# Releasing the first weight matrix earlier, moving one pair's keys and queries between the two weight loads, and summing keys on VectorE

## The chip, the cores and the metric

The kernel runs on one core of one Trainium2 chip. The metric is the device time of one execution in microseconds (us); lower is better. A profiled execution gives the span from the first to the last instruction, and the traces of the engines: TensorE (PE, with its weight loads as PEld), VectorE (DVE), ScalarE (ACT), GpSimd (POOL) and SyncE (SP), and of the DMA queues.

## The reference

Block-sparse causal attention is followed by a two-layer MLP with a GELU. Four batches (b), 8 heads, 768 positions, head size 64; the MLP takes 3072 rows of 512, with 2048 hidden columns.

```
k_rep = mean of k over blocks of 64 keys                  # 12 block means per head
gate  = q . k_rep, future blocks -1e9
sel   = the 3 best blocks of each query, and its own block
attn  = softmax(where(sel & causal, q.k / 8, -1e9)) . v
x     = attn, heads side by side                          # 3072 x 512
out   = gelu_tanh(x @ w_in) @ w_out                       # 512 -> 2048 -> 512
```

## The kernel before

Two heads make a *pair*; there are 16 pairs, numbered p = 0 to 15, four to a batch. For each pair the kernel loads keys, queries and values (k, q, v; 384 KB each), forms key sums of the 12 blocks, computes gate scores on TensorE, finds the third best with VectorE's MAX8 (`sel_e`), turns the result into an additive mask (`mask`, `mc`), multiplies keys with queries in six units per pair (`st_e`), takes exponentials on ScalarE (`ex_e`), zeroes the part above the diagonal on GpSimd (`af_e`), and multiplies with the values on TensorE (`pv_e`). Sums and quotients give `xn`, which is transposed to `xT`. When four pairs are through, the batch's MLP runs: `s1` (x times w_in, GELU into `G`) and `s2` (G times w_out). Batch 0 uses `pre` with transposes by TensorE and `heads2`; its second MLP half is `s2_plain`, 96 plain matmuls. Later batches use transposes by VectorE (`tr`) and `heads`.

Keys of batch 0 are transposed by TensorE into a PSUM bank (`turn`, lines 545 and 548). For the pairs named in `KSUM` (0 and 1 before) the transposing matmul against `identk` has 130 columns rather than 128, and the two more give the block sums; `ksb_h` then only has to multiply them with a mask. For the other pairs of batch 0, `ksb_h` has VectorE add up the transposed keys in the bank (TENSOR_REDUCE, line 583) before the mask.

Loads. SP issues nearly all loads, in one queue and in order. Batch 0's k, q and v come first; then come four `fill`s (8 small copies into `kT`), then `hold`, a copy of a few bytes out of the end of w_in into `after_in` (line 1567), which makes SP wait until w_in has landed; then the loads of pair 4 (k and q in four DMAs each, 96 KB each, line 400) and on. The two weight matrices are issued by POOL (`load_w`, line 460), two DMAs each. Ahead of w_in's stands a small copy by POOL that reads the v of pair 3, and so holds w_in back until that v has landed. w_out's two DMAs have no such copy before; they stand later in POOL's order.

Order. Every step is an `add`ed operation with a number. `ORDER` is a list of all numbers and is emitted as it stands, so it fixes each engine's own sequence. It was found ahead of time by a search over a plan with costs; `BUFFER` gives the PSUM and SBUF buffers in the order of use, and `ENGINE` moves single copies to ACT or POOL. `warm` operations (line 1524) are matmuls of zeros that nothing reads; a few of them stand wherever the plan had left TensorE unoccupied. An engine runs its own instructions strictly in order, so a wait of one holds up all behind it.

Of the kernel before, what the change touches and what calls it, by code (L numbers as in the profile page):

```python
# [189 lines left out]
    "POOL": [  # L190
        586, 587, 646, 647, 707, 972, 973, 1035, 1036, 1097, 1098,
        1159, 1160, 1425, 1489, 1551, 1612]}


class Op:
# [1431 lines left out]
```

## Time and profile before

| what | value |
|---|---|
| median of 3 runs | 257.9 us (257.89 to 257.94) |
| span of the profiled execution | 256.0 us |
| around the span (median less span) | 1.9 us |
| PE busy | 246.5 us, 96% of the span |
| DVE busy | 191.4 us, 75% |
| ACT busy | 176.4 us, 69% |
| POOL busy | 84.3 us, 33% |
| w_in issued, landed | 26.97, 41.55 us |
| first matmul with w_in, with w_out | 38.45, 50.31 us |

Times in the profile count from the first instruction. The page gives busy times of whole engines; the windows cut the span into stages; the timeline lists instructions with their start, duration, engine and line, and in square brackets the idle time before one and what ended it. The span is one execution and the median is of three others, so sums are made against the span, and what lies around it is added at the end.

### The profile page before, as it was taken

What the parts mean: (1) busy time and instruction counts of PE and PEld (TensorE: products, weight loads), DVE (VectorE), ACT (ScalarE), POOL (GpSimd) and SP (SyncE); (2) the same over time, 40 slices, a digit from 0 to 9 for tenths busy, and PEclk for the clock granted to TensorE, in tenths of its full rate; (3) what the DMA queues carried; (4) which work ended last, traced back from release to release, by engine and by line L of the source; (5) the groups of instructions that cost most, each with busy time, mean ns of one, the idle gap of its engine ahead of it and who ended that gap; (6) DMA issues with size and microseconds to landing.
All of it is one profiled execution on the core that took longest, in us unless ns stands there. A gap on an engine that the chain in (4) does not pass through costs nothing.

```text
span 256.0 us, 6451 instructions
## 1 busy us (share of the span) xinstructions
PE 246.5 (96%) x2485; PEld 171.2 (67%) x2485; DVE 191.4 (75%) x539; ACT 176.4 (69%) x225; POOL 84.3 (33%) x163
## 2 busy tenths in 40 slices
PE   7889999999998999999899999999999999999994
PEld 5667686555554566555578888555777786766883
DVE  2769751041989889989999999699889665579954
ACT  2399997634898998667969884566889957557300
POOL 8465970000239366223053853100056620000000
PEclk9999999999999999999999999999999999999999
DMA  8997599999989995999899699532112520040024
GB/s 164 218 208 166 94 212 191 213 161 157 184 142 165 153 143 99 172 179 199 127 174 110 144 188 166 118 94 69 26 34 72 64 74 1 3 165 0 3 82 164
DMA packets 130927, 32.62 MB, mean 127 GB/s; under 512 B 124528, under 2 KB 126928, under 8 KB 130896
## 3 DMA queue, kind: packets, MB, share of 16 engines
q1 hardware_dynamic: 126160, 27.62, 65.4%
q0 software_dynamic: 3136, 4.19, 9.7%
q10 hardware_dynamic: 1600, 0.39, 0.8%
q8 instruction: 19, 0.31, 0.5%
q14 instruction: 12, 0.10, 0.1%
HBM read 27.26 MB, written 6.29 MB: 131 GB/s over the span
## 4 chain that ended last, share of the span: by engine, by line
PE 51%; DVE 16%; SPq 11%; DMA 10%; POOL 4%; issue 3%; ACT 3%; ACTq 1%; DVEq 0%; POOLq 0%
PE bank L1372 17%; PE wide L1122 10%; SPq L400 9%; PE wide L1046 6%; PE wide L1211 5%; DMA w_in<-in_moe_w_in_dram 5%; PE bank L1085 5%; PE bank L1322 3%; DVE qT L367 3%; DMA sd<-in_k_dram 3%; DVE sel L719 2%; DVE s L564 2%; DVE XS L1309 2%; DMA G<-in_q_dram 2%; ACT ats L882 1%
## 5 line engine op out<-in xcount | busy, mean ns | idle before, releaser
L1122 PE MATMUL wide<-xT,w_in 128*128 128x384 f16 x416 | 72.6, 326 | 0.0
L1059 ACT ACTIVATE ats<-wide 128x896 f16<-128x896 f32 x72 | 63.4, 915 | 8.9 <-PE wide L1046 6.2
L1134 ACT ACTIVATE G<-wide 128x768 f16<-128x768 f32 x52 | 42.1, 810 | 27.3 <-PE wide L1122 27.0
L1122 PEld LDWEIGHTS <-w_in 128*128 128x128 f16 x416 | 40.0, 98 | 26.8 <-issue 1.3
L1073 POOL TENSOR_SCALAR_AFFINE_SELECT ats<-ats 128x256 f16<-128x256 f16 x72 | 33.3, 475 | 60.3 <-ACT ats L1059 60.2
L1046 PE MATMUL wide<-qT,kT 76*128 76x512 f16 (+3 forms) x192 | 39.1, 305 | 0.1
L564 DVE STREAM_TRANSPOSE s<-sd 128x768 f32<-128x768 f32 x24 | 23.1, 968 | 18.7 <-DMA sd<-in_k_dram 17.2
L1372 PE MATMUL bank<-w_out,G 128*128 128x256 f16 x216 | 31.4, 272 | 0.0
L1372 PEld LDWEIGHTS <-G 128*128 128x128 f16 x288 | 26.9, 98 | 6.0 <-issue 0.3
L1322 PE MATMUL bank<-w_out,G 128*128 128x512 f16 x96 | 28.1, 379 | 0.0
L365 POOL CAST kT<-s 64x768 f16<-64x768 f32 x17 | 15.2, 891 | 37.5 <-DVE s L564 37.0
L1421 DVE TENSOR_TENSOR osb<-bank,osb 128x512 f32<-128x512 f32 (+1 forms) x38 | 22.1, 592 | 5.1 <-PE bank L1372 4.5
L1085 PEld LDWEIGHTS <-ats 128*128 128x128 f16 x504 | 22.2, 98 | 3.9 <-POOL ats L1073 0.4
L1085 PE MATMUL bank<-v,ats 128*128 128x65 f16 x504 | 24.4, 194 | 0.2 <-POOL ats L1073 0.2
L1046 PEld LDWEIGHTS <-kT 76*128 76x128 f16 x192 | 17.3, 98 | 10.5 <-issue 0.8
L1372 PEld LDWEIGHTS <-XS 128*128 128x128 f16 x216 | 20.0, 98 | 5.5 <-DVE XS L1309 1.5
L1372 PE MATMUL bank<-TS,XS 128*128 128x256 f16 x144 | 22.0, 272 | 0.8 <-DVE XS L1309 0.7
L882 ACT ACTIVATE ats<-wide 128x1024 f16<-128x1024 f32 (+3 forms) x24 | 20.8, 924 | 1.3 <-PE wide L863 0.8
L365 POOL CAST v<-vsd 128x768 f16<-128x768 f32 x13 | 11.4, 875 | 13.8 <-DMA vsd<-in_v_dram 8.8
L969 DVE TENSOR_TENSOR xn<-bank,zr 128x384 f16<-128x384 f32 x24 | 13.4, 558 | 0.8
L719 DVE MAX8 sel<-sel 128x8 f32<-128x12 f32 x160 | 13.2, 158 | 0.6
L1322 PEld LDWEIGHTS <-G 128*128 128x128 f16 x96 | 8.9, 98 | 6.1 <-issue 0.3
(120 smaller groups left out, 358.6 us busy)
## 6 DMA issues: line engine op xcount, KB each, us to landing
out_dram<-osb SPq DMA_DIRECT2D x23, 256.0 KB
vsd<-in_v_dram SPq DMA_DIRECT2D x26, 192.0 KB
sd<-in_k_dram SPq DMA_DIRECT2D x48, 96.0 KB
sd<-in_q_dram SPq DMA_DIRECT2D x48, 96.0 KB
w_in<-in_moe_w_in_dram POOLq DMA_DIRECT2D x2, 1024.0 KB, 11.5
w_out<-in_moe_w_out_dram POOLq DMA_DIRECT2D x2, 1024.0 KB, 14.5
G<-in_k_dram SPq DMA_DIRECT2D x4, 192.0 KB
G<-in_q_dram SPq DMA_DIRECT2D x4, 192.0 KB
```

The source lines that it names most:

```text
L365: nc.gpsimd.tensor_copy(out=out, in_=in_)
L400: nc.sync.dma_start(out=T[key, p][64 * hh + 32 * a:64 * hh + 32 * a + 32], in_=SRC[key][b, 2 * hp + hh].rearrange("(t i) (a j) -> a i t j" ...
L564: nc.vector.transpose(out=T[key + "T32", p], in_=T[key, p].rearrange("p t j -> p (t j)"))
L882: nc.scalar.activation(out=T["at", u][:, :, 0:n], in_=plan.buf[("st",) + u].rearrange("p (h w) -> p h w", h=2)[:, :, 0:n], func=AF.Exp, bi ...
L1046: nc.tensor.matmul(st[:, x:e], kT16[i][h][0:76, s0:s0 + 128], qT16[i][h][0:76, s0 + (x - cb):s0 + (e - cb)], start=True, stop=True)
L1059: nc.scalar.activation(out=T["at", u][:, 0:n], in_=plan.buf[("st",) + u][:, 0:n], func=AF.Exp, bias=0.0, scale=SCALE)
L1073: nc.gpsimd.affine_select(out=dg, in_=dg, compare_op=ALU.is_ge, fill=0.0, base=0, pattern=[[0, 2], [1, 128]], channel_multiplier=-1)
L1085: nc.tensor.matmul(pvv[:, qc, 0:65], at[:, cb + (qc - jc) * 128: cb + (qc - jc + 1) * 128], v16[i][:, jc, h, :], start=(gi == 0 and jc == ...
L1122: nc.tensor.matmul(hps[:, 512 * e:512 * e + HALF], w_in16[:, ci, (2 * j + e) * 128: (2 * j + e + 1) * 128], T["xT", b][:, ci, HALF * h:HAL ...
L1134: nc.scalar.activation(out=G[:, :, h, j, :], in_=plan.buf["hps", b, j, h].rearrange("p (e w) -> p e w", e=2)[:, :, 0:HALF], func=AF.Gelu_a ...
L1322: nc.tensor.matmul(plan.buf["ops", b, ti], G[:, f % 2, 2 * ti // NC, f // 2, ti % (NC // 2) * 128:ti % (NC // 2) * 128 + 128], w_out16[:, ...
L1372: nc.tensor.matmul(dst[:, HD * h:HD * h + HD], FACT[m][0][:, j, t * 128:(t + 1) * 128], FACT[m][1][:, j, :], start=(clear and j == 0), sto ...
```

## The change

There are four edits.

1. `KSUM` becomes empty: keys of pairs 0 and 1 are transposed with 128 columns, and VectorE adds up their blocks, as for pairs 2 and 3.
2. w_in's copy on POOL reads the v of pair 2 rather than that of pair 3.
3. The loads go w_in, k and q of pair 4, w_out, v of pair 4, and on, rather than w_in, w_out, k, q, v of pair 4. `load_w` now puts a copy ahead of w_out too: it reads the q of pair 4, so that POOL issues w_out when that q has landed.
4. `ORDER`, `BUFFER` and `ENGINE` are searched anew.

```
-    KSUM = (0, 1)
+    KSUM = ()
...
-            if name == "in":
-                nc.gpsimd.tensor_copy(out=x, in_=T[after][96:97, 0, 1, 0:16])
+            src = T[after]
+            nc.gpsimd.tensor_copy(
+                out=x, in_=src[96:97, 0, 1, 0:16] if len(src.shape) == 4 else
+                src[96:97, 0, 0:16])
             for part in parts:
                 nc.gpsimd.dma_start(out=dst[part], in_=view[part])
...
-    for x in ('in', 'out', ('k', HP + 0), ('q', HP + 0), ('v', HP + 0), ('k', HP + 1), ('q', HP + 1), ('v', HP + 1)):
+    for x in ('in', ('k', HP), ('q', HP), 'out', ('v', HP), ('k', HP + 1), ('q', HP + 1), ('v', HP + 1)):
...
-            load_w(x, dst, src, parts, [ld[prev]] if x == "in" else
-                   [after_w["in", 0]], prio, prev)
+            load_w(x, dst, src, parts, [ld["v", 2], *chain] if x == "in"
+                   else [ld[prev], after_w["in", 0]], prio, ("v", 2) if x == "in" else prev)
```

What the new lists do, as read from the two orders side by side:

- SP's first DMA is half of pair 1's q (192 KB), ahead of pair 0's k. Of batch 0's loads, q and v of pair 3 come last, behind the v of pair 2.
- POOL: w_in's copy stands behind the cast of pair 1's v and ahead of the diagonal steps of pair 1 (before: behind the cast of pair 2's v). The cast of pair 3's v stands between diagonal steps of pair 2, with one of pair 2 and all four of pair 3 behind it. w_out's copy stands behind the last diagonal step of batch 0; after it come a cast of pair 4's k and steps of pairs 4 and 5.
- ACT: of the copies between the first and the last exponential of batch 0 there are 5 rather than 8; the others went to VectorE or ahead of the first exponential. One copy of `xT` behind the last exponential went to VectorE.
- TensorE: 72 `warm` matmuls rather than 39; 58 stand ahead of the first matmul of `s1` (before: 26), 13 from there to the MLP of batch 1, and 1 behind the last real matmul. The first `s1` group is one that needs w_in's second half (before: its first). 47 groups of `s1` (two matmuls each), the gate and the mask of pair 4, two `pv_e` steps of pair 3 and 4 warm matmuls stand ahead of the first `s2_plain` matmul.

More of the change, by code (lines that the diff above doesn't have):

```diff
@@ L21 @@
 ORDER = [
[134 rows of a table removed]
-BUFFER = [
[24 rows of a table removed]
[131 rows of a table added]
+BUFFER = [
[25 rows of a table added]
 ENGINE = {
     "ACT": [
[5 rows of a table removed]
[5 rows of a table added]
     "POOL": [
-        586, 587, 646, 647, 707, 972, 973, 1035, 1036, 1097, 1098,
-        1159, 1160, 1425, 1489, 1551, 1612]}
+        338, 587, 646, 647, 707, 708, 972, 973, 1035, 1036, 1097, 1098,
+        1159, 1160, 1425, 1426, 1488, 1489, 1551, 1612]}
 class Op:
```

324 rows, old and new, of tables (BUFFER, ENGINE, ORDER) are left out of this document.

## The prediction

> **What bounds the kernel now.** I read the page first, then the windows by stage, then the timeline at each stage's border.
>
> ```profile
> span 256.0 us, 6451 instructions
> PE 246.5 (96%) x2485; PEld 171.2 (67%) x2485; DVE 191.4 (75%) x539; ACT 176.4 (69%) x225; POOL 84.3 (33%) x163
> ...
> GB/s 164 218 208 166 94 212 191 213 161 157 184 142 165 153 143 99 172 179 199 127 174 110 144 188 166 118 94 69 26 34 72 64 74 1 3 165 0 3 82 164
> ```
>
> ```profile
> 12.50:38.45 25.95, 24.93 (x441) 18.59 (x441) 19.12 (x75) 23.97 (x34) 18.30 (x33) 1.00 0.95 170
> 38.45:69.60 31.15, 31.15 (x198) 17.79 (x196) 10.27 (x27) 18.95 (x26) 1.65 (x2) 1.00 1.22 182
> 69.60:101.66 32.06, 30.83 (x357) 18.36 (x354) 29.25 (x83) 29.10 (x37) 17.89 (x34) 1.00 0.93 140
> 101.66:135.00 33.34, 32.41 (x262) 20.90 (x259) 31.35 (x97) 24.26 (x33) 10.25 (x15) 1.00 1.18 169
> 160.00:252.70 92.70, 92.42 (x847) 67.71 (x844) 71.08 (x173) 57.54 (x69) 15.16 (x28) 1.00 0.25 63
> ```
>
> Each row has a stage, its length, and the busy time of PE, PEld, DVE, ACT and POOL. From 38.45 us on TensorE hardly rests: it is idle for 0, 1.23 and 0.93 us in the next three stages. So work on other engines counts only where it makes TensorE wait, and the change can win in two ways: `s1` starts earlier than 38.45, or one of those idle times goes. Until 38.45 the bound is another: ScalarE works 23.97 of 25.95 us, and what ends the stage is its last exponential.
>
> ```profile
> 12.50 1.03 ACT L882 ACTIVATE ats<-wide 128x1024 f16<-128x1024 f32 x1
> 34.82 3.26 ACT L882 ACTIVATE ats<-wide 128x1024 f16<-128x1024 f32 x4 [0.43 <-POOL ats L908]
> 38.45 1.79 PE L1122 MATMUL wide<-xT,w_in 128*128 128x384 f16 x10
> ```
>
> The exponentials of batch 0 run from 12.50 to 34.82 + 3.26 = 38.08 us, and `s1` follows at 38.45.
>
> The third thing to see is when the weights move.
>
> ```profile
> 23.50:28.50 5.00, 4.77 (x93) 3.61 (x92) 3.54 (x16) 4.98 (x8) 4.00 (x8) 1.00 0.13 30
> 28.50:40.50 12.00, 11.91 (x209) 9.02 (x210) 7.59 (x23) 10.62 (x15) 7.54 (x13) 1.00 1.10 191
> 52.50:69.00 16.50, 16.50 (x104) 9.07 (x103) 8.91 (x25) 9.00 (x12) 1.65 (x2) 1.00 1.17 172
> ...
> 25.94 0.83 POOL L365 CAST v<-TS 128x768 f16<-128x768 f32 x1
> 26.83 0.19 POOL L458 COPY after_in<-vsd 1x16 f32<-1x16 f32 x1
> 26.97 1.66 POOL L460 DMA_DIRECT2D w_in<-in_moe_w_in_dram  x2
> 34.74 1.78 POOL L460 DMA_DIRECT2D w_out<-in_moe_w_out_dram  x2
> ...
> 27.89 13.66 DMA w_in<-in_moe_w_in_dram
> 41.60 0.58 SPq L1567
> 43.41 2.70 SPq L400
> 46.15 3.21 SPq L400
> 49.40 2.79 SPq L400
> 53.12 0.54 SPq L400
> 53.70 0.52 SPq L400
> ...
> DMA to landing us min/median/max: 9.4/11.5/13.7
> ```
>
> The first three rows end in the DMA share and GB/s: for 5 us, until w_in moves, the queues carry 30 GB/s, then 191. w_in's two DMAs land 9.4 and 13.7 us after their issue, the second at 27.89 + 13.66 = 41.55. SP waits for that in `hold` and issues pair 4's keys only then, while w_out fills the queues: three of these DMAs of 96 KB hold SP for 2.70, 3.21 and 2.79 us, where one takes 0.54 once w_out is through. VectorE meanwhile has nothing to do:
>
> ```profile
> 54.40 0.98 DVE L564 STREAM_TRANSPOSE s<-sd 128x768 f32<-128x768 f32 x1 [14.96 <-DMA sd<-in_k_dram]
> 57.34 0.98 DVE L564 STREAM_TRANSPOSE s<-sd 128x768 f32<-128x768 f32 x1 [0.18 <-DMA sd<-in_q_dram]
> 69.64 0.90 ACT L1059 ACTIVATE ats<-wide 128x896 f16<-128x896 f32 x1
> 81.74 0.45 PE L756 MATMUL bank<-ident,madd 128*128 128x128 f16 x5 [1.20 <-DVE madd L724]
> ```
>
> It stands idle for 15 us before pair 4's keys come; at 69.60 to 101.66 it is busy 29.25 of 32.06 us, and TensorE's one long wait there (1.20 us at 80.5) is for pair 6's selection on VectorE.
>
> **Key sums on VectorE.**
>
> ```profile
> L583 DVE TENSOR_REDUCE ks<-bank 128x6 f32<-128x384 f32 x4 | 2.2, 550 | 0.8 <-ACT XS L363 0.8
> L545 PE MATMUL bank<-identk,G 128*128 128x130 f32 x24 | 3.5, 283 | 0.0
> L548 PE MATMUL bank<-identk,TS 128*128 128x128 f32 x12 | 1.7, 282 | 0.0
> 56.27 0.71 PE L1524 MATMUL bank<-XS 128*128 128x256 f16 x5
> 56.81 0.38 PE L1322 MATMUL bank<-w_out,G 128*128 128x512 f16 x1
> ```
>
> VectorE gets four more reductions of 0.55 us, 2.2 us in all. TensorE gets 12 transposes (1.7 us) for 24 matmul records (3.5), so it saves 1.8, and gets 33 warm matmuls at (56.81 - 56.27)/5 = 0.108, 3.6 us. Both lie nearly all ahead of `s1`, where TensorE is not the bound. On the path lie two of the reductions (1.1 us), and SP's first DMA, which puts pair 0's keys back by about 192 KB at 164 GB/s, 1.2 us. Against that, the first exponential of before stood behind copies on ScalarE that waited for VectorE's masked sums (2.1 and 1.6 us in the row quoted next). Bounds for the first exponential: 0.5 us earlier to 1.5 later; I take 0, since ScalarE's queue has slack there before and TensorE does the next transposes under the wait.
>
> **Batch 0's exponentials.** Three of ScalarE's eight copies between the first and the last exponential are gone:
>
> ```profile
> L363 ACT CAST XS<-bank 128x384 f16<-128x384 f32 x7 | 3.3, 490 | 4.3 <-DVE ksbx L595 2.1 <-DVE ksb L595 1.6 <-DVE ks L583 0.6
> ```
>
> 3 x 0.49 = 1.5 us at most; consecutive ones overlap a little, so I take 1.4. VectorE, which has 25.95 - 19.12 = 6.8 us to spare in the stage, hides them. With that cover gone (its chain to pair 3's mask is as long as ScalarE's) the gain is 0, and with pair 1's diagonals waiting behind w_in's copy on POOL it could be 1 us lost. Term: -1.4, between -1.9 and +1.0.
>
> **w_in.** All loads of batch 0 are through by 23.5. Pair 3's q and v (768 KB) now come behind pair 2's v, and at the page's 218 GB/s that is 3.6 us, so pair 2's v is moved at about 19.9; seen by POOL between then and 23.2 (the same 3.6 us ahead of the old copy at 26.83, rounded). I take 21.3, because the old copy stood behind a cast and not at the landing. Issue at 21.4 instead of 26.97 puts w_in's end at 41.55 - 5.5 = 36.0; sharing the queues with the last of pair 3's v and the fills costs perhaps 0.8, so 36.8. `s1` wants it at 38.45 - 1.4 = 37.05, now with its second half first. So the earlier w_in brings nothing by itself, but without it the 1.4 us would be lost: at the late bound (23.2) it lands at 38.7 and nothing is won. POOL's steps behind the waiting copy (pair 1's diagonals) wait until 23 us; the products that need them are due at about 23.5.
>
> By a rule of the Trainium skill ("SBUF — State Buffer", section "SBUF: two separate sides") a DMA issued from GpSimd has its descriptors written by GpSimd's cores, which are locked out while VectorE runs an operation that takes both ports; that speaks against issuing w_in in a stretch where VectorE works. The rows give 1.66 us for w_in's issue and 1.78 for w_out's, a difference of 0.12, and do not show such a lock. It is priced as a rival below.
>
> **Pair 4's keys and queries, then w_out.** `hold` ends at 36.8 + 0.6 = 37.4. Eight DMAs of 96 KB without w_out beside them take 0.55 to 0.85 each, 5.6 in all, to 43.0; the old queries landed at 57.2, 3 us behind their last issue with values behind them in the queue; at 172 GB/s the 768 KB take 4.6 us. So q lands at 44.5 to 46; I take 45.3. w_out is issued at 45.5; by w_in's 9.4 and 13.7 us its halves land at 54.9 and, from the second issue 0.9 later, 60.1. TensorE reaches the first `s2_plain` after 47 groups of `s1`; these cost 2 x 0.1624 each:
>
> ```profile
> 40.24 10.24 PE L1122 MATMUL wide<-xT,w_in 128*128 128x384 f16 x62
> 50.31 0.38 PE L1322 MATMUL bank<-w_out,G 128*128 128x512 f16 x1
> 66.69 2.10 PE L1322 MATMUL bank<-w_out,G 128*128 128x512 f16 x9
> 68.64 0.55 PE L1046 MATMUL wide<-qT,kT 76*128 76x512 f16 x3
> ```
>
> (50.31 - 40.24)/62 = 0.1624, so 15.3 us; gate, mask, two transposes, two products and four warm ones between them I estimate at 2.0 (the warm ones are 0.43 of it). 37.05 + 17.3 = 54.35, and w_out's first half is 0.6 us late. Term +0.6, from 0 to +6. The ninth `s2_plain`, the first to need the second half, comes 13 groups (4.2) and eight of (68.64 - 66.69)/9 = 0.217 later, 60.9: in time. In before, w_out was needed at 50.31 and TensorE did not wait.
>
> **The middle.** VectorE transposes and sums pair 4 at 42 to 47 us rather than 54 to 59, and the exponentials of batch 1 start at about 65 instead of 69.64 (60.9, four more groups of `s1`, and some 2.5 for the last GELU and the change of table), so the wait of 1.20 us for pair 6's selection should shrink; I take -1.0, from -1.2 to +1.0, as the search gives no promise of a new wait. Batch 1's sums: of 0.93 idle I take -0.3, from -0.9 to +0.8. After 160 us nothing is to be had: 0.28 us of idle time.
>
> **Sum.** 256.0 - 1.4 + 0.6 - 1.0 - 0.3 = 253.9; the median stands 1.9 above the span, so **255.8 us**, 0.8% below 257.9. About 0.2% (0.5 us) is what a measurement can tell from no change.
>
> **Rivals.**
> *w_out too late (slower).* Place: TensorE at its first `s2_plain`. POOL's copy waits for the queries, and each us that they land after 45 is one us of TensorE. It turns the gain at 47.4, where the wait is 2.7. If three of the eight DMAs take 3 us again (rows at 43.41 to 49.40), they land at 52, w_out's half at 61.5, the wait is 7: 256.0 - 1.4 + 7 - 1.3 + 1.9 = 262; halfway it is 259. For it: 0.6 us are missing already and all orders are fixed. Against: those rows are slow because w_out moved beside them. 0.20.
> *Pair 3's values starved (slower).* If w_in's packets start while over 200 KB of that v are left, these move at 96 KB in 3 us beside it and land after 29; POOL stands at the cast with the diagonals of pairs 2 and 3 behind it, and `s1` starts 3 to 5 us late: 259.5. For it: the same rows; against: the 3.6 us of q and v fit in POOL's way to the first packet. 0.08.
> *ScalarE isn't the bound ahead of `s1`.* The chain to pair 3's mask on VectorE, 2.2 us longer, keeps `s1` at 38.4; then -1.4 and +0.6 go: 256.0 - 1.3 + 1.9 = 256.6, or with the middle unchanged 257.9, so 257.5. 0.15.
> *Descriptors late.* If VectorE's work holds up both issues of w_in by 0.8 us each, `s1` waits 1.4 and w_out follows: 257.2 to 257.6. 0.07. By the Trainium skill's rule above this is what would happen; the trace so far bears it out only by 0.12 us.
> *All waits go.* 256.0 - 1.9 - 1.2 - 0.9 + 1.9 = 253.9. 0.08.
>
> **Numbers.** The forecast has 0.42 with a range of its own of 254.6 to 257.2. Faster: 0.42 + 0.08 + 0.04 from the two middle rivals, 0.54. Same: 0.14, nearly all theirs. Slower: 0.28 and 0.04 of theirs, 0.32. The range 253.8 to 259.6 leaves out the upper half of late w_out and some of the starved values at one end, a few hundredths at the other.
>
> **What would show it.** First exponential at 12 to 14 us, last one's end near 36.7; w_in issued at 21 to 22 and landed before 37.1; `s1` near 37; pair 4's keys at 0.55 to 0.85 us an issue; w_out issued near 45.5; TensorE idle at about 54 for less than 1 us; batch 1's first exponential near 65; `s1` of batch 1 near 100. The prediction is wrong if ScalarE idles over 2.5 us ahead of its last exponential, if TensorE waits over 2.7 us ahead of `s2_plain`, or if new idle time after 101 eats the rest.

## The result, and the profile after

The changed kernel takes 259.1 us (median of 13 runs) where the kernel before takes 257.8 in the same session: ratio 1.0058, 95% interval 1.0036 to 1.008. It is 0.6% slower; the prediction had it 0.8% faster. In a second session the ratio was 1.0058 again (1.0039 to 1.0077). The runs of the changed kernel spread over 258.1 to 260.9 us, those of before over 257.5 to 258.6.

The profiled execution of the changed kernel takes 259.66 us, 0.6 us above the median, and its span is 1.9 us longer than that of before. Its page and its windows, in the stages that the prediction used (length, then busy time of PE, PEld, DVE, ACT and POOL):

```profile
span 257.9 us, 6488 instructions
PE 249.0 (97%) x2506; PEld 172.8 (67%) x2506; DVE 193.0 (75%) x537; ACT 180.6 (70%) x228; POOL 85.8 (33%) x167
```

```profile
12.50:38.45 25.95, 25.15 (x429) 18.44 (x427) 21.26 (x87) 21.73 (x29) 14.94 (x25) 1.00 1.03 182
38.45:69.60 31.15, 31.15 (x238) 18.67 (x237) 13.76 (x35) 20.63 (x28) 4.55 (x8) 1.00 1.14 161
69.60:101.66 32.06, 32.03 (x361) 19.30 (x359) 25.39 (x77) 29.38 (x36) 17.21 (x33) 1.00 0.93 137
101.66:135.00 33.34, 33.05 (x264) 21.21 (x263) 31.71 (x93) 26.79 (x36) 11.86 (x18) 1.00 0.90 159
135.00:160.00 25.00, 24.10 (x307) 19.63 (x306) 22.03 (x43) 19.33 (x23) 11.97 (x24) 1.00 0.79 156
```

In the first row ScalarE works 21.73 us, 2.2 less than before, and VectorE 21.26, 2.1 more: the copies and sums moved as meant (the row is a fixed stretch of time; from the first exponential to the end of the last, ScalarE works 22.65 us instead of 23.61). In the third TensorE no longer rests (1.23 us before), in the fourth it rests 0.29 us (0.93 before); in the fifth 0.90 us of idle time are new in this execution. So the middle did what it should. The loss is ahead of all that. The timeline of ScalarE and TensorE of the changed kernel:

```profile
13.77 1.02 ACT L882 ACTIVATE ats<-wide 128x1024 f16<-128x1024 f32 x1 [0.30 <-PE wide L863]
39.32 1.30 ACT L882 ACTIVATE ats<-wide 128x256 f16<-128x256 f32 x2 [0.44 <-PE wide L863]
40.26 0.49 PE L1122 MATMUL wide<-xT,w_in 128*128 128x384 f16 x2
101.25 0.49 PE L1122 MATMUL wide<-xT,w_in 128*128 128x384 f16 x2
```

The first exponential comes at 13.77 (12.50 before), the last ends at 40.62 (38.08), `s1` starts at 40.26 (38.45; 37.05 was forecast). `s1` of batch 1 starts at 101.25, 0.41 us ahead of before: from one to the other the change gains 2.2 us. Now the start. TensorE's timeline of before, and then of the changed kernel; L545 and L548 are the transposes, L1524 the warm matmuls, L687 the first gate:

```profile
2.11 2.30 PE L1524 MATMUL bank<-XS 128*128 128x256 f16 x10
4.25 0.91 PE L545 MATMUL bank<-identk,G 128*128 128x130 f32 x6
4.99 0.49 PE L548 MATMUL bank<-identk,G 128*128 128x128 f32 x3
6.95 0.32 PE L687 MATMUL bank<-s,ksb 128*32 128x64 f32 x8
```

```profile
5.49 0.87 PE L548 MATMUL bank<-identk,G 128*128 128x128 f32 x3 [1.25 <-DMA G<-in_q_dram]
6.15 1.92 PE L1524 MATMUL bank<-XS 128*128 128x256 f16 x8
7.86 0.85 PE L548 MATMUL bank<-identk,G 128*128 128x128 f32 x3
8.50 1.06 PE L1524 MATMUL bank<-XS 128*128 128x256 f16 x4
9.35 0.95 PE L548 MATMUL bank<-identk,G 128*128 128x128 f32 x6
10.35 0.32 PE L687 MATMUL bank<-s,ksb 128*32 128x64 f32 x8
```

Read the rate from start to start. In before, three transposes take from 4.99 to 5.32, 0.11 us each. In the changed kernel TensorE waits 1.25 us for pair 0's queries, and behind that three transposes take from 7.86 to 8.50, 0.21 us each, and eight warm matmuls from 6.15 to 7.86, 0.21 each: half rate, until about 9.6 us. Before reached full rate at 4.3. Twelve warm matmuls at half rate stand between the transposes that the first gate needs; the gate is 3.4 us later than before's. The half rate was not in the prediction at all.

### The profile page after: what moved, and what is told of

Read it like the earlier page. It is cut to its first block, busy times and chain, and to the rows that moved or that the text cites. A ratio compares the mean times of both kernels' runs of the same rounds, so it can differ in the third digit from the quotient of the medians.

```text
span 257.9 us, 6488 instructions
## 1 busy us (share of the span) xinstructions
PE 249.0 (97%) x2506; PEld 172.8 (67%) x2506; DVE 193.0 (75%) x537; ACT 180.6 (70%) x228; POOL 85.8 (33%) x167
## 4 chain that ended last, share of the span: by engine, by line
PE 80%; DVE 13%; ACT 2%; DMA 2%; issue 1%; POOL 0%; ACTq 0%; DVEq 0%
PE wide L1122 24%; PE bank L1372 18%; PE wide L1046 9%; PE bank L1322 8%; PE bank L1085 5%; PE wide L1211 5%; DVE XS L1309 2%; PE wide L863 2%; DVE sel L719 2%; PE bank L687 2%; PE bank L1524 2%; PE bank L931 2%; DMA G<-in_q_dram 2%; DVE sel L710 1%; PE bank L548 1%; PE bank L988 1%
## 5 line engine op out<-in xcount | busy, mean ns | idle before, releaser
L1122 PE MATMUL wide<-xT,w_in 128*128 128x384 f16 x416 | 73.7, 326 | 0.0
L1134 ACT ACTIVATE G<-wide 128x768 f16<-128x768 f32 x52 | 42.0, 809 | 25.6 <-PE wide L1122 25.5
L1073 POOL TENSOR_SCALAR_AFFINE_SELECT ats<-ats 128x256 f16<-128x256 f16 x72 | 32.0, 457 | 54.0 <-ACT ats L1059 50.0
L1372 PE MATMUL bank<-w_out,G 128*128 128x256 f16 x216 | 32.2, 272 | 0.9 <-DVE osb L1421 0.9
L1372 PEld LDWEIGHTS <-G 128*128 128x128 f16 x288 | 27.0, 97 | 7.6 <-issue 1.2
L1322 PE MATMUL bank<-w_out,G 128*128 128x512 f16 x96 | 28.1, 379 | 0.0
L363 POOL CAST kT<-s 64x768 f16<-64x768 f32 x20 | 17.3, 865 | 20.1 <-DVE s L564 19.7
L1372 PE MATMUL bank<-TS,XS 128*128 128x256 f16 x144 | 22.6, 272 | 0.1
L1524 PE MATMUL bank<-XS 128*128 128x256 f16 x72 | 17.1, 326 | 1.1 <-DVE ks L302 1.1
L703 DVE STREAM_TRANSPOSE sel<-bank 128x160 f32<-128x160 f32 (+2 forms) x17 | 5.5, 330 | 14.7 <-PE bank L687 14.5
## 6 DMA issues: line engine op xcount, KB each, us to landing
out_dram<-osb SPq DMA_DIRECT2D x23, 256.0 KB
```

The costliest lines, as they stand in the source:

```text
L363: nc.gpsimd.tensor_copy(out=out, in_=in_)
L1073: nc.gpsimd.affine_select(out=dg, in_=dg, compare_op=ALU.is_ge, fill=0.0, base=0, pattern=[[0, 2], [1, 128]], channel_multiplier=-1)
L1122: nc.tensor.matmul(hps[:, 512 * e:512 * e + HALF], w_in16[:, ci, (2 * j + e) * 128: (2 * j + e + 1) * 128], T["xT", b][:, ci, HALF * h:HAL ...
L1134: nc.scalar.activation(out=G[:, :, h, j, :], in_=plan.buf["hps", b, j, h].rearrange("p (e w) -> p e w", e=2)[:, :, 0:HALF], func=AF.Gelu_a ...
L1322: nc.tensor.matmul(plan.buf["ops", b, ti], G[:, f % 2, 2 * ti // NC, f // 2, ti % (NC // 2) * 128:ti % (NC // 2) * 128 + 128], w_out16[:, ...
L1372: nc.tensor.matmul(dst[:, HD * h:HD * h + HD], FACT[m][0][:, j, t * 128:(t + 1) * 128], FACT[m][1][:, j, :], start=(clear and j == 0), sto ...
```

## The experiments

Each ran beside the kernel before on one chip; the ratio is to that, with its interval. "First selection" is the end of pair 0's first `madd` on VectorE (9.65 in before, 12.28 in the changed kernel). Starts and ends (of `s1`, say) are read from one profiled execution; times are medians over several.

**The start: late keys, warm matmuls or the rate?** `k0_first`, a move in SP's order:

```
 ORDER of the changed kernel
-    0, 22, 1890, 1891, 9, ... 1, 1902, 12, 1903, 71,
+    0, 1890, 1891, 9, ... 1, 1902, 12, 22, 1903, 71,
```

> The changed kernel with pair 0's keys first in SP's queue and the first half of pair 1's queries behind them, nothing else moved. Theory A (the start is late because the first keys are): pair 0's keys are turned about 1 us earlier, the first exponential comes at about 12.8 instead of 13.77 us, s1 at about 39.2 instead of 40.26, and the time is 258.0, 1.0 below the changed kernel's. Theory B (VectorE's key sums are the start's and the stage's limit): the keys come earlier but the sums of pairs 0 to 3 remain, s1 gains 0.4 at most, time 258.7. Theory C (warm matmuls stand ahead of TensorE's steps): nothing moves, 259.1.

258.3 us, 1.003 (1.0009 to 1.005). TensorE waited only 0.34 us ahead of its first transpose, ran at full rate from 4.8 us, the first selection ended at 9.42 and `s1` started at 38.39, earlier than theory A expected. But both the keys and the rate had changed, and the time fell by less than `s1` did. TensorE's timeline of it shows the next wait:

```profile
4.57 0.58 PE L548 MATMUL bank<-identk,G 128*128 128x128 f32 x3 [0.34 <-DMA G<-in_q_dram]
56.90 0.38 PE L1322 MATMUL bank<-w_out,G 128*128 128x512 f16 x1 [1.19 <-DMA w_out<-in_moe_w_out_dram]
```

`few_warm` takes warm matmuls out:

```
 ORDER of the changed kernel
-    44 warm numbers, 1904 to 1947 (from the first transpose to s1)
```

> The changed kernel without 44 of the 58 warm matmuls ahead of s1; the 14 ahead of its first transpose stay. Theory C (warm matmuls hold up TensorE's steps): they cost 44 times 0.11 to 0.2 us, so some of ScalarE's 4.5 us of idle time behind the units' matmuls goes; s1 about 1.5 earlier, 257.6. Theories A and B: they only fill time in which TensorE waits; s1 within 0.3 of 40.26, 259.1. Third case: without them the granted clock falls below 1.00 in the first 12 us or later, and s1 comes 1 us or more later, 260.

259.38 us, 1.0079 (1.0064 to 1.0093). With nothing to fill its waits TensorE stayed at half rate until 12 to 13.5 us. Yet `s1` came at 39.31, 0.95 us earlier, as no half-rate warm matmul stood ahead of the needed ones; the first `s2_plain` then waited 1.20 us for w_out. So theory C has a part in it, and the third case's lower rate too, and neither alone is the cause.

`bridge` keeps the late keys and all warm matmuls, and only moves ten of them:

```
 ORDER of the changed kernel
-    12, 1903, 71, 1904, 15, 23, 1905, ...
+    12, 1903, 1904, 1905, ... 1913, 71, 15, 23, ...
```

> The changed kernel with ten of its warm matmuls moved from behind the first transposes to ahead of them, so that TensorE works through the 1.25 us in which it waited for pair 0's queries; SP's order is the changed kernel's. Theory A1 (TensorE ran at half rate until 9.6 us because it had stood idle from 4.03 to 5.49; 128-column transposes 0.213 us from start to start there, 0.109 behind it): full rate comes by 6 us, the first gate at about 8.6 instead of 10.35, the first exponential near 12.0, s1 near 38.8; time 258.2. Theory A2 (only the late keys count, the rate does not): the first gate stays within 0.5 us of 10.35, s1 near 40, time 259.

258.5 us, 1.0032 (1.0011 to 1.0052). TensorE's timeline of it, the exponentials', and `s1`:

```profile
2.11 3.30 PE L1524 MATMUL bank<-XS 128*128 128x256 f16 x19
5.59 0.96 PE L548 MATMUL bank<-identk,G 128*128 128x128 f32 x6 [0.18 <-DMA G<-in_q_dram]
8.54 0.32 PE L687 MATMUL bank<-s,ksb 128*32 128x64 f32 x8
11.97 1.02 ACT L882 ACTIVATE ats<-wide 128x1024 f16<-128x1024 f32 x1 [0.29 <-PE wide L863]
37.90 0.49 PE L1122 MATMUL wide<-xT,w_in 128*128 128x384 f16 x2
56.74 0.38 PE L1322 MATMUL bank<-w_out,G 128*128 128x512 f16 x1 [1.52 <-DMA w_out<-in_moe_w_out_dram]
```

The data come no earlier (5.59), but full rate was there at 4.3, the first gate at 8.54, the first exponential 1.8 us and `s1` 2.36 us earlier, as A1 said. SP's order costs through the wait that it opens and what stands behind that wait: `k0_first`, with data 1 us earlier, has `s1` 0.5 us later than `bridge`. Two things changed at once, though: the wait is closed, and ten warm matmuls no longer stand between the needed transposes. The time falls by 0.3% only; in this profile w_out is now late by 1.52 us.

`after_again` is the changed kernel once more, for a second profile.

> The changed kernel, unaltered, beside the two below on one chip. If TensorE's rate at the start is what makes its runs spread (258.1 to 260.9): in this profile half rate ends between 9 and 10 us again where TensorE waited over 1 us for pair 0's queries, with s1 at 40 to 40.5 and a time of 259 to 260; in an execution whose half rate ends by 7 us, s1 is at 38 to 39 and the time 258.1 to 258.5. If the rate isn't it: s1 near 40.3 whichever it is.

259.29 us, 1.0058. Half rate to 9.2 us behind a wait of 1.32 us, first selection at 12.18, `s1` at 40.82: the first profile was no exception. No profile of an execution near 258.1 was had, so whether the spread of the times comes from the moment of full rate is not shown.

`before_gap` puts the fault into the kernel before:

```
 ORDER of before
-    1898, 1899, 1900, 1901, 1902, 1903, 1904, 62,
+    1898, 62,
```

> The kernel before without the last six of the 15 warm matmuls ahead of its first transpose, so that TensorE stands idle for the 1.28 us from 2.96 to 4.25, as it did for 1.25 us in the changed kernel; nothing else differs, and no data come later. Theory A1 (the idle time itself keeps TensorE at half rate): 128-column transposes stay at 0.213 us until 7 to 9.5 us (4.3 in before), the first gate is 1.0 to 1.5 us later than 6.95, and whatever of it the wait for VectorE at 8.5 to 9.7 does not swallow reaches s1: first selection (madd) up to 1.2 us later than 9.65, time 257.9 to 259.0. Theory A2 (the rate is not a matter of that idle time): half rate ends at 4 to 5.7 us as in the other runs of before's start, first gate within 0.3 us of 6.95, 257.7.

258.06 us, 1.0013 (1.0004 to 1.0022). TensorE's timeline of it (with a shorter list, its lines stand seven higher: L538 and L541 are the transposes, L680 the gate):

```profile
4.47 1.64 PE L538 MATMUL bank<-identk,G 128*128 128x130 f32 x6 [1.30 <-DMA G<-in_k_dram]
5.90 0.85 PE L541 MATMUL bank<-identk,G 128*128 128x128 f32 x3
7.75 0.44 PE L680 MATMUL bank<-s,ksb 128*32 128x64 f32 x8
```

The same idle time, with all loads as in before: half rate until 8.4 us, the gate 0.80 us later, the first selection 0.66 and `s1` 0.67 us later (10.31 and 39.12). So the idle time alone makes the half rate last. It costs before less, 0.3 us of time. Before has two warm matmuls and not twelve between the first transposes, and a wait for VectorE that can swallow some; that these are the reason is argued, not tested.

**Key sums.** `before_sums_dve` makes edit 1 alone, `sums_pe` and `k0_sums_pe` undo it alone:

```
 before:            -    KSUM = (0, 1)    +    KSUM = ()
 changed, k0_first: -    KSUM = ()        +    KSUM = (0, 1)
```

> The kernel before with one edit of the change alone: KSUM = (), so VectorE adds up the keys of pairs 0 and 1 as well; order, buffers and loads are those of before. Theory B (VectorE's key sums): the first exponential comes about 1 us later than 12.50, pair 3's mask 1 to 2 us later than 31.1, s1 1 us or more later than 38.45; time 258.8 or more. Theories A and C: VectorE had 6.8 us to spare in that stage, s1 moves by less than 0.3, 257.8.

259.37 us, 1.0066 (1.0044 to 1.0088): `s1` at 40.80, over 1 us later, as theory B had it. Its windows:

```profile
12.00:15.00 3.00, 1.52 (x20) 1.13 (x18) 2.72 (x9) 2.02 (x5) 0.48 (x1) 1.00 1.39 218
15.00:20.00 5.00, 4.82 (x49) 3.12 (x41) 2.55 (x15) 3.54 (x6) 3.89 (x10) 0.66 1.26 206
```

The granted clock falls to 0.66 at 15 to 20 us, behind 3 us in which TensorE worked half the time. Of its six executions the two with a mean clock of 1.000 took 258.05 and 258.84 us, the four with a lower one 258.84 to 259.97. Was it that?

`before_sums_warm` fills those gaps:

```
 ORDER of before with KSUM = ()
+    33 warm numbers: 6 ahead of 73, 10 ahead of 84, 3 ahead of 78, 5 ahead of 86, 9 ahead of 102
```

> The kernel before with VectorE's key sums for all pairs, as in before_sums_dve, and 33 more warm matmuls of zeros in the gaps that the smaller transposes leave on TensorE ahead of 15 us. Theory R (what the key sums on VectorE cost there is TensorE's rate, which fell to half at 15 to 20 us): full rate stays to s1, s1 within 0.8 us of 38.45, time 257.8 to 258.3 against 259.37. Theory V (it is VectorE's 2.2 us of reductions on its chain to pair 3's mask): s1 40 or later, time 259 to 259.5.

260.54 us, 1.0106 (1.0093 to 1.0119). Full rate from 3.8 us to `s1`, granted clock 1.00, and still `s1` at 41.61. Theory R's forecast fell, but the run does not clear the rate. The added warm matmuls stand in the way themselves: pair 1's selection ends at 20.11 (17.62 in `before_sums_dve`, 16.77 in before), and VectorE waits 1.01 and 1.45 us for TensorE ahead of it. From there to pair 2's selection (26.18; 25.37 in `before_sums_dve`, 23.02 in before) it takes 6.1 us at full rate, as in before (6.3), where `before_sums_dve` with its clock of 0.66 took 7.8. So of the 2.4 us by which pair 2's selection is late in `before_sums_dve`, some 0.9 came with the sums up to pair 1's selection and some 1.5 with the lower rate behind it. Both have a part.

> The changed kernel with KSUM = (0, 1) again: TensorE's matmuls against identk give the block sums of pairs 0 and 1, and VectorE's four reductions of 0.55 us go. Theory A (late first keys): first exponential about 0.4 us earlier, s1 40.0, time 258.8. Theory B (VectorE's key sums): VectorE's chain to pair 3's mask is 2.2 us shorter and that mask, which came at 33.02, comes at about 31; s1 at 38.5, time 257.4. Theory C (warm matmuls): no change or 0.3 slower, as TensorE gets 1.8 us of work ahead of s1.

260.15 us, 1.0088 (1.0061 to 1.0114): slower by more than any of the three theories had it. TensorE had the same half rate to 9.9 us, in which each matmul against `identk` costs 0.21.

> Pair 0's keys first on SP and KSUM = (0, 1) again, so that TensorE is at full rate when it forms the sums. Theory B' (VectorE's sums cost where TensorE is at full rate; in sums_pe the half rate hid it: 12 matmuls of 0.213 us more before the first gate): VectorE's chain to pair 3's mask is 1 to 2.2 us shorter than in k0_first, s1 at about 37.2 instead of 38.39, first s2_plain then waits about 2.4 us for w_out, time 257.9 to 258.3. Theory S (the searched order hides the sums): s1 38.2 to 38.6, 258.3.

258.74 us, 1.0036 (1.0015 to 1.0058), `s1` at 39.25 against 38.39 in `k0_first`; half rate lasted to about 6 us in this profile. From pair 0's selection to pair 3's it takes 21.2 us against 21.7 in `k0_first`, 0.4 us shorter where B' had 1 to 2.2. So in the searched order VectorE's sums cost next to nothing, and theory B' fell. Edits 1 and 4 go together: the first alone costs 0.7% in before's order, part of it by the rate, and the searched order makes room for it.

**w_in.** `k0_win_v3` undoes edit 2, `before_win_v2` makes it alone:

```
 k0_first: -   ..., ("v", 2) if x == "in" else prev)     +   ..., ("v", 3) if x == "in" else prev)
 before:   -   [after_w["in", 0]], prio, prev)           +   [after_w["in", 0]], prio, ("v", 2) if x == "in" else prev)
           and 157 moves ahead of 43 in ORDER
```

> Pair 0's keys first on SP, and w_in's copy reads the v of pair 3 again, at the same place in GpSimd's order. If the earlier release is worth something once s1 is on time: w_in is issued 1.5 to 3 us later (23.5 to 25) and lands 38 to 39.5, s1 waits up to 1 us, k and q of pair 4 and w_out come as much later, and the first s2_plain waits 3 to 4 us instead of 1.2; time 260 to 261. If it is worth nothing: 258.3, s1 within 0.3 us of 38.39.

262.69 us, 1.0193 (1.0168 to 1.0218), longer than either case had it. GpSimd's timeline:

```profile
25.43 0.20 POOL L456 COPY after_in<-vsd 1x16 f32<-1x16 f32 x1 [3.68 <-DMA vsd<-in_v_dram]
25.97 1.67 POOL L460 DMA_DIRECT2D w_in<-in_moe_w_in_dram  x2 [0.34 <-issue]
```

The copy waits 3.68 us at its new place, and GpSimd's diagonals stand behind it; TensorE waited 2.56 us for one at 28.4. `s1` came at 42.01, w_in landed at 40.11, q of pair 4 and w_out followed. The loss is the queue behind the waiting copy more than the weights.

> The kernel before with one edit of the change alone: w_in's copy reads the v of pair 2 and stands ahead of GpSimd's cast of pair 1's v, 3.5 us earlier in its order. As the prediction had it (the earlier w_in brings nothing by itself, as the exponentials set s1): w_in lands at about 37.5 to 38.5 and s1 stays at 38.4; hold and pair 4's keys come 3 to 4 us earlier, which may take up to 1.2 us off the wait for pair 6's selection; time 256.8 to 257.8. Rival (pair 3's v and GpSimd's casts are held up by w_in): s1 1 us or more later, 259.

259.67 us, 1.0082 (1.0065 to 1.01): the rival. In its profile (of an execution of 261.74 us, the longest of six) GpSimd waited too (1.08 us, and the issue behind it), TensorE waited 2.39 us for its diagonals at 27.4, pair 3's selection ended at 33.98 instead of 30.08 and `s1` started at 42.35. An earlier release is worth something only with an order of GpSimd that was made for it.

**w_out.** `k0_s2_late` moves five groups:

```
 ORDER of k0_first
-    347, ... 433, 416, 368, 434, 435, 369, 370, ... 371,
+    347, ... 416, 368, 369, 370, 371, 433, 434, 435, ...
```

> Pair 0's keys first on SP, as in k0_first, and five more groups of s1 (5 times 0.325 us) ahead of the first s2_plain. Theory W (with s1 on time TensorE waits 1.19 us for w_out's first half at 56.90): the wait goes or falls below 0.2 us, later stages come 1.2 us earlier, time 257.1 against 258.3 of k0_first. Rival: the wait turns up again at the next groups, because GELU or w_out's second half (62.6) is the next in line; then time 258.0 to 258.3.

258.02 us, 0.9994 (0.9981 to 1.0007): the same as before. The wait is gone (L1322, the `s2_plain` matmul, starts at 57.43 straight behind the groups; w_out's half landed at 55.76), later stages come 1.1 us earlier than in `k0_first`. The time fell 0.3 us rather than 1.2; this profile had half rate until 6.6 us and `s1` at 38.65.

`bridge_s2_late` and `k0_bridge_s2_late` put the mended parts together (ten warm matmuls moved, or four and the keys first).

> The changed kernel with two orders mended: ten warm matmuls ahead of the first transposes (as in bridge) and five more groups of s1 ahead of the first s2_plain (as in k0_s2_late); SP's order is the changed kernel's. Theory (rate at the start and w_out are the two faults and add up): full rate by 5 us, s1 at about 37.9, no wait of over 0.3 us at the first s2_plain, time 258.5 - 1.3 = 257.2, that is 0.2% below before. Rival (they don't add: with s1 earlier, GELU or w_out's second half holds TensorE next): 258.0 to 258.5.

258.74 us, 1.0034 (1.0017 to 1.0051): no better than `bridge`. In its profile ten warm matmuls at half rate made the first transpose late (6.16), half rate lasted to 7.0, and `s1` came at 38.96; `bridge`, with the same start, had full rate at 4.3.

> As the kernel above, but pair 0's keys also first on SP, and only four warm matmuls moved ahead of the first transposes. If the earlier keys help beside the full rate: first gate about 0.9 us earlier, s1 at about 37.4, time 256.8. If pair 1's queries then come as much later as pair 0's keys come earlier (TensorE waited 0.66 us for them in k0_first): s1 37.9 to 38.4, time 257.2 to 257.6.

257.7 us, 1.0001 (0.9988 to 1.0015), `s1` at 38.38. This takes the whole loss back; it does not beat before.

`wout_first` undoes edit 3 in it (the loads' places in `ORDER` move with it):

```
-    for x in ('in', ('k', HP), ('q', HP), 'out', ('v', HP), ...
+    for x in ('in', 'out', ('k', HP), ('q', HP), ('v', HP), ...
```

> k0_bridge_s2_late with the load order of before: w_out behind w_in (GpSimd issues it at about 36, with pair 3's diagonals), then pair 4's keys and queries, and so with the third edit undone. If the middle's gain is this edit's: pair 4's keys and queries hold SP for 2.7 to 3.2 us each again, the queries land at 52 to 56 instead of 45, TensorE waits 2 us or more for pair 4's mask or later for pair 5's or 6's; time 259 to 261. If the middle's gain is the searched order's alone: no wait over 0.5 us there, no wait for w_out either; time 257.4 to 257.7.

266.15 us, 1.0326 (1.0292 to 1.036), 5 us more than the first case had. SP's and TensorE's timelines:

```profile
37.23 10.85 SPq L398 DMA_DIRECT2D sd<-in_k_dram  x4
57.73 0.76 PE L687 MATMUL bank<-s,ksb 128*32 128x160 f32 x8 [5.80 <-DVE s L564]
```

Pair 4's four key DMAs hold SP for 10.85 us (0.58, 0.98, 4.11 and 5.04), where they take 2.44 in the changed kernel, and TensorE waits 5.8 us for pair 4's gate. The middle's gain hangs on the load order, in an order that counts on early keys.

**What else bounds batch 0.** Even at full rate the exponentials take 26.3 us in `bridge` and 27.0 in `k0_bridge_s2_late`, 25.6 in before. `acts` takes work off VectorE:

```
 ENGINE of k0_bridge_s2_late
-    "ACT": [..., 121, 331, ...]
+    "ACT": [..., 121, 130, 134, 141, 331, ...]
 and 373, 374, 375, 376 ahead of 433 in ORDER
```

> k0_bridge_s2_late with three copies of pair 3's keys and queries on ScalarE, as in the kernel before, rather than on VectorE, and four more groups of s1 ahead of the first s2_plain. Theory D (VectorE is the bound of batch 0 in the changed order: from 11 to 31 us it rests less than 1 us): its chain loses up to 1.5 us, pair 3's selection (madd) ends at about 29.7 instead of 31.08, the last exponential at about 37.6, s1 at about 37.3, time 256.7 against 257.7. Rival (TensorE or ScalarE takes the bound at once, since both have little room from 18 to 30): selection within 0.4 us of 31.08, s1 within 0.4 us of 38.38, time 257.4 to 257.9.

258.5 us, 1.0031 (1.0016 to 1.0045). The windows of `k0_bridge_s2_late` and of `acts`, and VectorE in `acts`:

```profile
11.50:31.00 19.50, 18.61 (x309) 13.37 (x303) 17.74 (x70) 15.72 (x21) 11.31 (x19) 1.00 1.14 206
```

```profile
11.50:31.00 19.50, 18.32 (x300) 13.07 (x294) 16.47 (x64) 16.30 (x23) 11.28 (x19) 1.00 1.13 204
```

```profile
28.06 0.20 DVE L949 RECIPROCAL zr<-bank 128x6 f32<-128x6 f32 x1 [0.85 <-PE bank L931]
```

VectorE lost 1.3 us of work and now waited for TensorE; pair 3's selection came at 31.80 and `s1` at 39.10, each 0.7 us later. Theory D fell; the rival's 0.4 us was exceeded too.

`lean` takes work off TensorE:

```
 ORDER of k0_bridge_s2_late
-    28 warm numbers, 1922 to 1949
```

> k0_bridge_s2_late without the 28 warm matmuls that stand from about 12 us to the first groups of s1 (0.107 us each from start to start at full rate, 3.0 us in all); those ahead of 12 us stay. If warm matmuls stand in the way of TensorE's steps in batch 0 at full rate (TensorE is busy 18.61 of the 19.50 us from 11.5 to 31): pair 3's selection ends 0.5 to 1.5 us ahead of 31.08, s1 at 37.2 to 37.9, time 256.9 to 257.4 against 257.7. If they fill time in which TensorE would wait for VectorE or ScalarE: s1 within 0.2 us of 38.38, 257.7. If they hold the rate up: some transposes of 128 columns at 0.213 us again between 12 and 38, s1 39 or later, 258.5 or more.

259.12 us, 1.005 (1.0036 to 1.0064). Pair 3's selection ended 0.53 us and the exponentials 0.66 us earlier, as the first case had it, and no transpose behind 12 us was at half rate. But `s1` came at 38.65, as it waited 0.77 us for w_in, which landed at 38.61 in this profile (36.15 in `k0_bridge_s2_late`), and `s2_plain` waited 0.85 and 1.39 us for w_out's halves. w_in was issued only 0.5 us later; why it took longer is not shown. So the warm matmuls do stand in the way by about half a us there, and late weights took more than that back. What else orders the hand-offs of VectorE and TensorE in batch 0 was not resolved further.

**The last stretch.** The windows from the last batch's `s1` to TensorE's end, of before and of the changed kernel:

```profile
208.02:252.70 44.68, 44.65 (x352) 33.78 (x349) 32.19 (x54) 19.29 (x23) 0.00 (x0) 1.00 0.14 52
```

```profile
208.15:254.20 46.05, 45.82 (x375) 34.69 (x371) 32.90 (x57) 21.65 (x27) 0.35 (x1) 1.00 0.18 54
```

`tail_before` takes before's order from there:

```
 ORDER and ENGINE of k0_bridge_s2_late
-    everything behind the 1427th of its operations other than warm ones (s1 of batch 3)
+    the same operations in the order and on the engines of before, with four warm numbers
```

> k0_bridge_s2_late up to the last batch's MLP (about 206 us), and from there the order, engines and four warm matmuls of the kernel before. If the last stretch is where the changed order gave its middle's gain back (TensorE idle 0.62 us longer from 206 us to its end, and 0.4 us more behind its last matmul): that stretch is 1.0 us shorter, time 256.7 against 257.7. If those us come from what the earlier stages left to do (1.4 us of matmuls more in the last stretch) and not from its order: 257.5 to 257.8.

258.71 us, 1.004 (1.0026 to 1.0053), the stretch 46.8 us long (46.0 in `k0_bridge_s2_late`), with a wait of 0.68 us of its own. It is not the order of the stretch: the second row has 23 matmuls more than the first, which counts four warm ones; 20 products of `pv_e` are among them. Part of what the middle gained was only put off to the end.

## Why the prediction was wrong

**The first exponential** ("I take 0", bounds -0.5 to 1.5) was the step that failed first: it came 1.27 us late, inside the bounds, and the first selection came 2.63 us late. The working saw the late DMA and the longer path on VectorE and let "TensorE does the next transposes under the wait" pay for both. The wait itself was the cost. It left TensorE at half rate for four more us, with twelve warm matmuls, priced at 0.108 us, at 0.214 on the path. `before_gap` shows the wait alone: the first selection 0.66 us later. `bridge`, which closes the wait and moves ten of these matmuls ahead of it, takes back 1.80 us of the first selection; `few_warm`, which takes them out at half rate, 1.26. How the loss divides between the rate and the place of these matmuls is not separated.

**Batch 0's exponentials** (-1.4, as VectorE had "6.8 us to spare in the stage") failed second, and by more: from the first exponential to the end of the last it took 26.85 us instead of 25.58, +1.3. ScalarE did lose 1.0 us of work there, but its idle time, all of it waiting for TensorE's units, went from 2.0 to 4.2 us and ate the saving. The end goes with pair 3's selection, the last `madd` of the batch on VectorE (before, then the changed kernel):

```profile
29.56 0.53 DVE L724 SCALAR_TENSOR_TENSOR madd<-sel,ownm 128x120 f16<-128x120 f32 x1
```

```profile
32.67 0.28 DVE L724 SCALAR_TENSOR_TENSOR madd<-sel,ownm 128x120 f16<-128x120 f32 x1
```

The last exponential ends 8.0 us behind the end of this step in before and 7.7 in the changed kernel. In the other runs with before's order it is 8.0 as well, in those with the changed order 7.5 to 7.7, and 8.2 in `k0_win_v3`. From the first selection to pair 3's it takes 20.4 us in before and 20.7 in the changed kernel. So the end of the stage goes with the selections, and a lighter ScalarE did not bring these earlier: the first selection is 2.63 us late, the last exponential's end 2.54. That was the rival "ScalarE isn't the bound ahead of `s1`", given 0.15 and priced at no loss. The spare us of VectorE's mean were no cover, and `before_sums_dve` shows that the sums of two more pairs in the wrong place cost 1.7 us of time, part of it by the rate. Together the two steps put the last exponential's end 3.9 us behind the forecast and `s1` 3.2 us (40.26 against 37.05), as `s1` now starts 0.36 us ahead of that end and not 0.37 behind it. The forecast's own sign of being wrong, ScalarE idle for over 2.5 us, is there: 4.0 us in seven waits for TensorE's units between the first and the last.

**w_in** held within its bounds: issue 22.52 (21.4 forecast), landing at 37.18 (36.8). The issue took 1.66 us, as before, beside a VectorE at work; the rival of the late descriptors, and the rule of the Trainium skill ("SBUF — State Buffer", "SBUF: two separate sides") behind it, did not show here. That the release is needed held too, in the changed order (`k0_win_v3`), though by another way: what waits is GpSimd's queue. The rival "pair 3's values starved" did not come.

**w_out** (+0.6) was hidden in the changed kernel, as `s1` was late by more. GpSimd's timeline (the first row is the issue of w_in, named above):

```profile
22.52 1.66 POOL L460 DMA_DIRECT2D w_in<-in_moe_w_in_dram  x2
46.47 0.23 POOL L456 COPY after_out<-sd 1x16 f32<-1x16 f32 x1 [5.38 <-DMA sd<-in_q_dram]
46.92 1.78 POOL L460 DMA_DIRECT2D w_out<-in_moe_w_out_dram  x2 [0.22 <-issue]
```

The queries land at 46.4 rather than 45.3, w_out's first half at 57.22, and the first `s2_plain` starts at 57.42. With `s1` on time the wait is 1.19 (`k0_first`) to 1.52 us (`bridge`): mechanism right, size two to two and a half times the 0.6.

**The middle** (-1.0 and -0.3) was right: -1.20 and -0.64 of idle time, though batch 1's first exponential came at 68.2 us (69.2 in before) and not near 65. **Behind it** the forecast had nothing. The last stretch is 1.4 us longer, with the 23 matmuls that were put off, and 0.4 us more lie behind TensorE's last matmul; in this execution 0.90 us of idle time at 135 to 160 came on top. So from `s1` to the span's end the change gains nothing (+0.1 us), where -0.7 was forecast, and the loss of 1.8 us at `s1` stands as it is. The sum: 256.0 + 1.8 + 0.1 = 257.9, the span. In the profile of `after_again` that idle time is not there: `s1` is 2.4 us late, the span 257.7, and behind `s1` the change gains 0.7 us. That this is the forecast's -0.7 is luck: the wait for w_out (+0.6) did not arise, the stretch from `s1` to `s1` of batch 1 gained 2.2, and the end cost 1.8.

That 259.1 us lies in the stated range is luck too. It stands there for late w_out (259) and for starved values (259.5), and neither came.

## What to carry to other kernels

Near a kernel's start, a short wait of TensorE is priced not by its length but by the rate behind it: read the rate from start to start of equal matmuls, and place filling matmuls ahead of a wait, not behind it. A saving on the engine that looks like the bound is worth what the hand-offs let through, and the spare time of another engine over a stage is no cover for a step on the path. When one wait is taken away, look up what lands next: here w_out stood 0.2 us behind a delay of 1.8.

## What the runs showed of the hardware

TensorE's half rate at the start does not show in the granted clock: the windows say 1.00 while transposes take 0.213 us from start to start instead of 0.109. Full rate came by 3.8 to 7.0 us in the 15 profiles where TensorE had worked from 1.07 us up to it without a wait of 1 us, at 8.5 to 9.9 in the four with one wait of 1.2 to 1.3 us, and at 13.5 in one with a wait of 1.08 us and shorter ones behind it (`few_warm`). The Trainium skill ("TensorE: Matmul & The Clock Gate", "Part 1: The HAM clock gate") has the array at half clock until a free-running window of about 3.4 us has been busy; the runs agree in that one and the same start goes to full rate at another moment from execution to execution (4.3 us in `bridge`, 7.0 in `bridge_s2_late`), but the earliest, 3.8, is only 2.7 us behind TensorE's first matmul. The Trainium skill's table (same page, "Why this matters for your kernels") warns of idle gaps above about 3 us in mid-kernel. Before full rate a shorter one counts: 1.30 us put it off from 4.3 to 8.5 us (`before_gap`).

Beside w_out, some of the DMAs of 96 KB hold SP for 2.7 to 5.0 us, whichever pair's they are: pair 4's keys in `wout_first`, and in the changed kernel pair 5's queries (0.60, 2.71, 4.39 and 4.39 us); VectorE waits 3.41 us for them at 64.86, off the path:

```profile
37.85 2.44 SPq L398 DMA_DIRECT2D sd<-in_k_dram  x4
47.95 12.22 SPq L398 DMA_DIRECT2D sd<-in_q_dram  x4
64.86 0.98 DVE L564 STREAM_TRANSPOSE s<-sd 128x768 f32<-128x768 f32 x1 [3.41 <-DMA sd<-in_q_dram]
```
